# Delta-rule recurrence, soft MoE and FFN in one kernel: keys, queries and values loaded and scattered per step, held by semaphores, instead of per pair of steps

## The chip, the cores and the metric

The kernel runs on one core of a Trainium2 chip. The metric is the device time of one execution in microseconds (us), as the median over runs.

## The reference

Three layers follow each other. The first one is the part that the change touches:

```python
# q, k, v: (4, 8, 768, 48), beta: (4, 8, 768); D = 48, 32 heads in all
k_n = k / (norm(k) + 1e-06)
state = zeros(B, H, D, D)
for t in range(768):
    y[t] = q[t] @ state
    state += beta[t] * outer(k_n[t], v[t] - k_n[t] @ state)
x = y as (3072, 384)
logits = x @ phi                      # 32 slots, 4 for each of 8 experts
d = softmax(logits over the tokens);  slots = d.T @ x
slots[e] = relu(slots[e] @ w1[e]) @ w2[e]
x = softmax(logits over the slots) @ slots
out = max(0.01 * h, h) @ w_out        # with h = x @ w_in
```

## The kernel before

The 768 positions are cut into 24 steps (`NST`) of 32 positions, for all 32 heads at once. Inside a step the recurrence is a triangular system, so that each step is a row of small matrix products with one solve; the solves are made on VectorE (DVE) for four steps at a time (`solve`, six groups), ahead of the steps that use them. The heads are in two halves, A = 0 and A = 1.

**Loads.** The inputs lie in DRAM by pairs of steps. `load_pair(p)` brings keys and queries of two steps, twice: as a block-diagonal operand (`kbd`, in the arena; two scatters of 192 KB, L161) and as a plain one (`kqr`, 768 KB, L162). `gram(s)` multiplies one by the other (L172, 32 small matmuls a step), ScalarE (ACT) copies one half of the product (L178), and DVE masks the other (L183). Grams run eight to ten steps ahead of the step that uses them. `load_kv(p)` brings keys and values of two steps (768 KB, L276). `step_k(p)` scales the keys of both steps on ACT and splits them into two 16-bit parts (L302, L305, L306), and `step_kdma(p)` scatters them into `khb`, the operand of the state's update (four transfers of 96 KB for a pair, L314). `step_dma(s)` scatters the solved matrices into `tmb` (four of 64 KB, L325) and loads `kqb`, keys and queries of one step once more (two of 192 KB, L321).

**One step.** TensorE (PE) forms keys times state (`ks_mm`, L347) into `ksu`, to which the values have been added (L339). ACT and DVE split it (`z_of`, L361 to L363). PE multiplies by the solved matrix (`u_mm`, L369: T z, closed in steps 0 to 16 by a further matmul, L376), ACT reads u (L374, L377), and PE adds keys times u to the state's accumulator in PSUM (`s_mm`, L390: the state's products). ACT reads the new state (L393), which the next step's `ks_mm` needs. The step's output y is queries times state (`qs_mm`, L355) plus L400. This loop from state to state is the chain of a step; grams, the solve of a later group, the outputs' logits and the loads lie beside it.

**What sets the order.** A scheduler orders each engine's instructions ahead of time, by priorities in a table `P`; on the chip each engine runs its list in order and waits on semaphores. All transfers are issued from one queue, SyncE's (SP), in one order; each issue also waits for the transfer eight before it. PE, ACT, DVE, POOL and SP each have a program of their own, and loading of code is done by transfers too (the page calls these queues "instruction").

**Stages.** 0 to 17 us: first loads and a warm-up of PE. 17 to 49 us: grams of steps 0 to 7 and the first solve's start. 49 to 74 us: the first solve on DVE. 78 to 352 us: the 24 steps. 352 to 418 us: the experts' weights arrive. 418 to 647 us: the FFN (L898, L930 to L938), which loads nothing large.

Of the kernel before, what the change touches and what calls it, by code (L numbers as in the profile page):

```python
# [24 lines left out]
ROWS = 3  # L25
GALT = 8
WARM = 28
KB = 2
GR = ((0, 2, 2), (2, 0, 0))
COLS = 2  # L30
NL = 7
# [16 lines left out]
def fused_kernel(ctx: ExitStack, tc: tile.TileContext, kq, kv, bu, phi, w1, w2, wi, wo, out):  # L48
    nc = tc.nc
    ve, sc, gp, pe, sy = nc.vector, nc.scalar, nc.gpsimd, nc.tensor, nc.sync  # L50

    def pool(stack, name, bufs, **kw):
        return stack.enter_context(tc.tile_pool(name=name, bufs=bufs, **kw))
# [7 lines left out]
    p_late = pool(ctx, "late", 2, side="right")  # L61
# [34 lines left out]
    def place(kb, shape, dt):  # L96
# [6 lines left out]
        if len(shape) == 2:  # L103
# [46 lines left out]
    last_dma = [None]  # L150
    kqc, gcs, mms, tcs, nns, kvs, vns = {}, {}, {}, {}, {}, {}, {}

    def load_pair(p):
        n = 4 if p < 4 else 2
        c, kb = kqc[p] = kqr[p % n], kbd[p % n]
        kr = kq[p].rearrange("p k (b x y) -> p k b x y", b=2, x=2)
        cr = c[0:96].rearrange("p k b x i h -> p k (b x i h)")
        for ks in (slice(0, 1), slice(1, 2)) if p == 0 else (slice(0, 2),):
            for sl in range(2):
                q, i = slice(48 * sl, 48 * sl + 48), slice(32 * sl, 32 * sl + 32)  # L160
                last_dma[0] = sy.dma_start(kb[q, ks, :, i].rearrange("p k b i h -> p k b (i h)"), kr[q, ks, :, 0]).ins  # L161
            sy.dma_start(cr[:, ks], kq[p, :, ks])  # L162

    def gram(s):
        k = s % 2
# [104 lines left out]

    solved = {}

    def load_kv(p):
        t = p_late.tile([128, 2, 2, 384], F32, tag=f"kv{p % 2}", name="kv", bufs=1)
        with tc.issue_after(kb_dma[0]) if p < 2 else nullcontext():
            sy.dma_start(t, kv[p])  # L276
        kvs[p] = t

    khs = {}

    def step_m(s):
        g, k = divmod(s, 4)
# [6 lines left out]
    def step_ew(s):  # L289
        g, k = divmod(s, 4)  # L290
        v1 = kvs[s // 2][:, s % 2, 1]
        if s % 2:
            kvs.pop(s // 2)
        vs = p_w.tile([128, 8, 48], F32, tag="vs", name="vs", bufs=3)
        gp.tensor_tensor(vs, v1.rearrange("p (h e) -> p h e", h=8), nns[g][:, k].unsqueeze(2).to_broadcast([128, 8, 48]), MULT)  # L295
        vns[s] = vs

    def step_k(p):
        khc = p_w.tile([128, 2, 2, 384], F16, tag="khc", name="khc", bufs=KB)
        for k in range(1 if p == NST // 2 - 1 else 2):  # L300
            k1 = kvs[p][:, k, 0]
            sc.activation(k1, k1, AF.Copy, scale=64.0)  # L302
            kv1 = k1.rearrange("p (d a h) -> p a d h", a=2, h=4)
            k0, kl = [khc[:, k, l].rearrange("p (a d h) -> p a d h", a=2, h=4) for l in range(2)]
            sc.activation(k0, kv1, AF.Copy)  # L305
            gp.tensor_tensor(kl, kv1, k0, SUB)  # L306
        khs[p] = khc.rearrange("p k l (a x) -> p (k l a) x", a=2)

    def step_kdma(p):
        khc = khs.pop(p)  # L310
        n = 1 if p == NST // 2 - 1 else 2
        for b in range(4):
            q, o = slice(32 * b, 32 * b + 32), 48 * (b % 2)
            last_dma[0] = sy.dma_start(khb[q, 0:n, :, :, b // 2, o:o + 48, :].rearrange("p k l a d h -> p (k l a) (d h)"), khc[q, 0:4 * n]).ins  # L314

    def step_dma(s):
        g, k = divmod(s, 4)
# [11 lines left out]
    sps = [t[:, 0:384].rearrange("p (b h e) -> p b h e", b=2, h=4) for t in spf]  # L329
# [6 lines left out]
    last_u = {}  # L336
# [48 lines left out]
    def s_mm(s, A, u):  # L385
        kb = khb[:, s % 2]
        for hh in range(4):
            for i, (a, b) in enumerate(PASSB):
                for bp in range(2):
                    pe.matmul(sps[A][:, bp, hh, :], kb[:, a, A, bp, :, hh], u[:, b, hh, :],  # L390
                              start=False, stop=(s == NST - 2 and i == 2), skip_group_check=True)
        st = p_s.tile([128, 2, 4, 48], F32, tag=f"s{A}", name="st")
        sc.activation(st.rearrange("p b h e -> p (b h e)"), sps[A].rearrange("p b h e -> p (b h e)"), AF.Copy)  # L393
        S[A] = st
# [170 lines left out]
    wm = ps_m.tile([128, 512], F32, tag="m", name="wm")  # L565
    for i in range(WARM):
        pe.matmul(wm, one16, xg[0][:, 0].rearrange("p a b -> p (a b)")[:, 0:512], start=True, stop=True)
    for p in range(2):
        load_pair(p)
    with tc.issue_after(last_dma[0]):  # L570
        sy.dma_start(beta, bu)
    for s in range(4):
# [1 line left out]
    kb_dma = [last_dma[0]]  # L574
    with tc.issue_after(last_dma[0]):
        load_kv(0)
        phi_sb = p_sm.tile([128, 3, 32], F32, tag="pt", name="phi_sb")
        sy.dma_start(phi_sb, phi)
    sc.activation(phs[:, 0], phi_sb, AF.Copy, scale=64.0)
# [1 line left out]
    late_zero()  # L581
    bs.add(solve(0))
    bs.run(8)
    for p in range(2, 4):
        load_pair(p)
    for p in range(2, 4):
        bs.run(8)
        for t in range(2 * p, 2 * p + 2):
            drain(gram(t))
            bs.run(8)  # L590
    bs.run()
    load_kv(1)
    prep(0)
    step_k(0)
    step_kdma(0)
    step_dma(0)
    prep(1)
    load_pair(4)
    bs.add(solve(1))
    bs.run(DQ[0])  # L600

    for s in range(NST):
        y = ps_y.tile([128, 8, 48], F32, tag="y", name="y")
        z, u = {}, {}
# [49 lines left out]
        if s < NST - 1:  # L654
            with pri("st"):
                s_mm(s, 0, u[0])
# [5 lines left out]
        if s < NST - 1:  # L662
            with pri("st"):
                s_mm(s, 1, u[1])
        if s + 2 < NST:
            if s % 2 and (s + 3) // 2 < NST // 2:
                load_kv((s + 3) // 2)
            with pri("prep"):
                prep(s + 2)
        if s % 2 and s + 1 < NST:  # L670
            with pri("dma"):
                step_kdma((s + 1) // 2)
        if s % 2 == 0 and s + 2 < NST:
            with pri("prep"):
                step_k(s // 2 + 1)
        conv()
        bs.run(dq[6])
        bg.run(GR[s % 2][2])
# [4 lines left out]
        with pri("x"):  # L683
            x = xg[s // 4 % 2][:, s % 4]
# [5 lines left out]
            else:  # L690
                ve.scalar_tensor_tensor(x1, y, 2.0 ** -8, x0, MULT, SUB)
        vns.pop(s)
        if s % 2 == 0 and (s + 10) // 2 < NST // 2:
            with pri("split"):
                load_pair((s + 10) // 2)
        if s % 4 == 2:
            bs.run()
            if s == 14:
# [153 lines left out]
    with tc.high_priority(offset=CHAIN_PRIO):  # L852
# [132 lines left out]
```

## Time and profile before

| | us |
|---|---|
| median of three runs | 650.26 |
| the three runs | 647.53, 650.26, 650.75 |
| the profiled execution's own time | 649.27 |
| its span in the trace | 647.5 |

The page gives the busy time of each engine, the clock that PE was granted, and how the DMA engines were used. The chain of waits follows the last instruction back to what released it; in it "issue" is a stretch in which PE waited for nothing that the trace shows. The timelines show each engine's instructions with the idle time ahead of them and what ended it. The windows give each engine's busy time in a stretch.

### The profile page before, as it was taken

What the parts mean: (1) busy time and instruction counts of PE and PEld (TensorE: products, weight loads), DVE (VectorE), ACT (ScalarE), POOL (GpSimd) and SP (SyncE); (2) the same over time, 40 slices, a digit from 0 to 9 for tenths busy, and PEclk for the clock granted to TensorE, in tenths of its full rate; (3) what the DMA queues carried; (4) which work ended last, traced back from release to release, by engine and by line L of the source; (5) the groups of instructions that cost most, each with busy time, mean ns of one, the idle gap of its engine ahead of it and who ended that gap; (6) DMA issues with size and microseconds to landing.
All of it is one profiled execution on the core that took longest, in us unless ns stands there. A gap on an engine that the chain in (4) does not pass through costs nothing.

```text
span 647.5 us, 21565 instructions
## 1 busy us (share of the span) xinstructions
PE 545.4 (84%) x9171; PEld 388.5 (60%) x9171; DVE 400.0 (62%) x1064; ACT 300.2 (46%) x714; POOL 205.1 (32%) x217
## 2 busy tenths in 40 slices
PE   5651399899999898989777757778999999999996
PEld 2640287778788787878776222345655555555553
DVE  3169988769676797978366895699333333233321
ACT  0322246456456456655343221255565556555652
POOL 9432003023033123131111000054555554555452
PEclk9875599899899899989888687899999999999999
DMA  8972247748475655487969999520010101010101
GB/s 212 256 154 98 35 117 167 169 117 193 101 157 125 148 119 133 84 222 157 258 167 364 416 412 416 204 97 1 1 51 0 50 1 50 0 51 1 50 1 49
DMA packets 67184, 87.46 MB, mean 135 GB/s; under 512 B 41520, under 2 KB 58160, under 8 KB 66032
## 3 DMA queue, kind: packets, MB, share of 16 engines
q1 hardware_dynamic: 67088, 86.09, 48.0%
q8 instruction: 72, 1.18, 0.8%
q14 instruction: 24, 0.20, 0.1%
HBM read 70.53 MB, written 4.72 MB: 116 GB/s over the span
## 4 chain that ended last, share of the span: by engine, by line
PE 65%; DMA 12%; DVE 12%; issue 6%; ACT 2%; SPq 1%; POOL 0%; DVEq 0%; ACTq 0%
PE ops L898 27%; PE gm L172 7%; PE sps L390 5%; PE y L355 4%; PE ksu L347 4%; PE hps L930 3%; PE ksu L369 3%; PE y L400 3%; DMA we<-in_w_dram 2%; PE ksu L339 2%; DMA arena<-in_w_dram 2%; DMA arena<-in_kq_dram 2%; DMA khb<-khc 2%; DVE arena L256 2%; DVE arena L242 2%
## 5 line engine op out<-in xcount | busy, mean ns | idle before, releaser
L938 POOL TENSOR_TENSOR gl<-gf,gh 128x512 f16<-128x512 f32 x96 | 114.0, 1204 | 171.2 <-ACT gh L937 100.8
L898 PE MATMUL ops<-late,gh 128*128 128x384 f16 x768 | 143.6, 326 | 0.3 <-ACT gh L937 0.3
L936 DVE SCALAR_TENSOR_TENSOR gf<-hps,hs 128x512 f32<-128x512 f32 x96 | 62.2, 686 | 112.6 <-ACT hs L935 107.5
L898 PEld LDWEIGHTS <-gh 128*128 128x128 f16 x768 | 74.9, 98 | 56.6 <-ACT gh L937 3.0
L898 PE MATMUL ops<-late,gl 128*128 128x384 f16 x384 | 81.2, 326 | 1.6 <-POOL gl L938 1.5
L172 PE MATMUL gm<-kqr,arena 128*32 128x64 f32 x1280 | 56.0, 309 | 29.4 <-DVE er L213 24.6
L935 ACT ACTIVATE hs<-hps 128x512 f32<-128x512 f32 x96 | 52.4, 594 | 51.9 <-PE hps L930 51.9
L937 ACT ACTIVATE gh<-gf 128x512 f16<-128x512 f32 x96 | 60.3, 630 | 32.5 <-DVE gf L936 27.3
L295 POOL TENSOR_TENSOR vs<-kv,nn 128x384 f32<-128x384 f32 x24 | 21.8, 913 | 145.1 <-PE ksu L339 117.2
L172 PEld LDWEIGHTS gm<-kqr,arena 128*32 128x32 f32 x1280 | 43.3, 150 | 35.3 <-DVE er L213 25.1
L390 PE MATMUL sps<-u,khb 128*128 128x48 f16 x1104 | 52.7, 195 | 5.5 <-issue 2.1
L256 DVE TENSOR_TENSOR arena<-arena 128x81 f32<-128x81 f32 (+12 forms) x150 | 55.7, 371 | 0.2
L390 PEld LDWEIGHTS <-khb 128*128 128x128 f16 x1104 | 46.6, 118 | 11.8 <-issue 10.2
L898 PEld LDWEIGHTS <-gl 128*128 128x128 f16 x384 | 37.4, 98 | 26.8 <-POOL gl L938 2.4
L260 DVE TENSOR_TENSOR arena<-arena 128x81 f32<-128x81 f32 (+12 forms) x150 | 49.7, 331 | 0.0
L242 DVE SCALAR_TENSOR_TENSOR arena<-arena 128x28 f32<-128x28 f32 (+27 forms) x186 | 49.2, 275 | 0.4
L355 PE MATMUL y<-st,kqb 128*32 128x48 f32 x1472 | 39.7, 233 | 1.0 <-issue 1.0
L347 PE MATMUL ksu<-st,kqb 128*32 128x48 f32 x1472 | 37.3, 233 | 3.3 <-issue 2.4
L347 PEld LDWEIGHTS ksu<-st,kqb 128*32 128x32 f32 x1472 | 30.8, 158 | 9.8 <-issue 6.1
L393 ACT ACTIVATE st<-sps 128x384 f32<-128x384 f32 x46 | 22.4, 490 | 29.8 <-PE sps L390 29.7
L369 PE MATMUL ksu<-z,tmb 128*128 128x48 f16 x576 | 28.7, 193 | 8.7 <-issue 7.8
L306 POOL TENSOR_TENSOR khc<-kv,khc 128x384 f16<-128x384 f32 x23 | 21.4, 952 | 45.9 <-ACT khc L305 45.9
(171 smaller groups left out, 891.6 us busy)
## 6 DMA issues: line engine op xcount, KB each, us to landing
we<-in_w_dram SPq DMA_DIRECT2D x22, 768.0 KB, 13.5
kqb<-in_kq_dram SPq DMA_DIRECT2D x50, 192.0 KB, 5.4
kv<-in_kv_dram SPq DMA_DIRECT2D x12, 768.0 KB, 7.2
arena<-in_w_dram SPq DMA_DIRECT2D x10, 768.0 KB, 11.9
kqr<-in_kq_dram SPq DMA_DIRECT2D x9, 768.0 KB, 7.8
tmb<-tc SPq DMA_DIRECT2D x96, 64.0 KB, 3.3
arena<-in_wi_dram SPq DMA_DIRECT2D x8, 768.0 KB, 7.6
raw<-in_wo_dram SPq DMA_DIRECT2D x8, 768.0 KB, 9.2
```

What stands on the lines that cost most here:

```text
L172: pe.matmul(gm[32 * b:32 * b + 32, h, :], kb[:, k, bp, r, h], c[:, k, bp, :, :, h], start=(h == 0), stop=True, skip_group_check=True)
L242: ve.scalar_tensor_tensor(R[:, i, 0:j], R[:, j, 0:j], gu[:, i, j:j + 1], R[:, i, 0:j], MULT, ADD)
L256: ve.tensor_tensor(tv, gu[:, j + 2:, j:j + 1].to_broadcast([128, n, w]), R[:, j:j + 1, 0:w].to_broadcast([128, n, w]), MULT)
L260: ve.tensor_tensor(R[:, j + 2:, 0:w], R[:, j + 2:, 0:w], tv, ADD)
L347: pe.matmul(ksu[A][32 * b:32 * b + 32, 48 * hh:48 * hh + 48], kb[:, bp, 0, r, 4 * A + hh], st[:, bp, hh, :], start=False, stop=True, skip_ ...
L355: pe.matmul(y[32 * b:32 * b + 32, 4 * A + hh, :], kb[:, bp, 1, r, 4 * A + hh], st[:, bp, hh, :], start=(A == 0 and hh == 0), stop=False, s ...
L390: pe.matmul(sps[A][:, bp, hh, :], kb[:, a, A, bp, :, hh], u[:, b, hh, :], start=False, stop=(s == NST - 2 and i == 2), skip_group_check=True)
L898: pe.matmul(ops[t], g[:, 128 * t:128 * t + 128], w, start=(ft == 0 and i == 0), stop=(ft == 15 and i == 2))
L935: sc.activation(hs, hps, AF.Copy, scale=2.0 ** -12)
L936: ve.scalar_tensor_tensor(gf, hps, 0.01 * 2.0 ** -12, hs, MULT, MAX)
L937: sc.activation(gh, gf, AF.Copy)
L938: gp.tensor_tensor(gl, gf, gh, SUB)
```

## The change

Everything that was loaded for a pair of steps is loaded for one step, with half the size and the same sum of bytes: `load_pair` becomes `load_kq` (two scatters of 96 KB and one load of 384 KB for a step), `load_kv` takes one step (384 KB), and `step_k` and `step_kdma` treat one step (four scatters of 48 KB). In the loop the scatters for step s+10 wait for the last product of the state in step s (`s_mm`, half 1), and the values of step s+3 wait for the last matmul of T z in step s (`u_mm`, half 0). `khc` gets a third buffer, each half as large. Before the loop, the second `step_k` is made ahead of the first step. Matmuls, ACT and DVE instructions are the same in number; SP issues 88 transfers more.

```diff
-KB = 2
+KB = 3
...
-    def load_pair(p):
+    def hold(dma, ins):
+        tc.add_manual_dep(dma.ins, ins.name, mybir.DependencyInfo(mybir.DependencyClass.Sync, mybir.DependencyReason.DATA), reason="hold")
+
+    def load_kq(s, ins=None):
+        p, k = divmod(s, 2)
         n = 4 if p < 4 else 2
-        c, kb = kqc[p] = kqr[p % n], kbd[p % n]
...
+        for sl in range(2):
+            q, i = slice(48 * sl, 48 * sl + 48), slice(32 * sl, 32 * sl + 32)
+            d = sy.dma_start(kb[q, k, :, i].rearrange("p b i h -> p b (i h)"),
+                             kq[p, q, k].rearrange("p (b x y) -> p b x y", b=2, x=2)[:, :, 0])
+            if ins is not None:
+                hold(d, ins)
+            last_dma[0] = d.ins
+        sy.dma_start(c[0:96, k].rearrange("p b x i h -> p (b x i h)"), kq[p, :, k])
...
-    def load_kv(p):
-        t = p_late.tile([128, 2, 2, 384], F32, tag=f"kv{p % 2}", name="kv", bufs=1)
-        with tc.issue_after(kb_dma[0]) if p < 2 else nullcontext():
-            sy.dma_start(t, kv[p])
-        kvs[p] = t
+    def load_kv(s, ins=None):
+        p, k = divmod(s, 2)
+        if k == 0:
+            kvs[p] = p_late.tile([128, 2, 2, 384], F32, tag=f"kv{p % 2}", name="kv", bufs=1)
+        d = sy.dma_start(kvs[p][:, k], kv[p, :, k])
+        if ins is not None:
+            hold(d, ins)
...
-    for p in range(2, 4):
-        load_pair(p)
+    for t in range(4, 8):
+        load_kq(t)
...
-    load_kv(1)
+    load_kv(2)
     prep(0)
     step_k(0)
     step_kdma(0)
     step_dma(0)
     prep(1)
-    load_pair(4)
+    step_k(1)
+    load_kq(8)
+    load_kq(9)
...
+        if s + 3 < NST:
+            load_kv(s + 3, last_u[0].ins)
         if s + 2 < NST:
-            if s % 2 and (s + 3) // 2 < NST // 2:
-                load_kv((s + 3) // 2)
             with pri("prep"):
                 prep(s + 2)
-        if s % 2 and s + 1 < NST:
+        if s + 1 < NST - 1:
             with pri("dma"):
-                step_kdma((s + 1) // 2)
-        if s % 2 == 0 and s + 2 < NST:
+                step_kdma(s + 1)
+        if s + 2 < NST - 1:
             with pri("prep"):
-                step_k(s // 2 + 1)
+                step_k(s + 2)
+        if s + 10 < NST:
+            load_kq(s + 10, last_s[0])
...
-        if s % 2 == 0 and (s + 10) // 2 < NST // 2:
-            with pri("split"):
-                load_pair((s + 10) // 2)
```

The change moves instructions at three places. In the rows below the lines of the changed kernel are higher: L185 was L178 (copy of a gram), L190 was L183 (mask of a gram), L216 was L209, L220 to L223 were L213 to L216, L230 was L223 (rows of the solve), L308 and L311 were L302 and L305 (keys), L366 and L367 were L361 and L362 (z), L379 and L382 were L374 and L377 (u), L398 was L393 (state), L319 was L314, L326 was L321, L330 was L325, L164 was L161 and L284 was L276 (transfers).

DVE, start of the first solve, before (`mm` is a masked gram, `er`, `br` and `arena` belong to the solve):

```order
L202 STREAM_TRANSPOSE arena<-arena 128x1024
L209 TENSOR_SCALAR t_367<-arena 128x32
L183 TENSOR_TENSOR mm<-gm,causal 128x2x4x32 x2
L213 TENSOR_SCALAR er<-nu 128x32
L233 RECIPROCAL ru<-nu 128x32
L214 TENSOR_TENSOR er<-er,arena 128x32
L215 RECIPROCAL er<-er 128x32
L183 TENSOR_TENSOR mm<-gm,causal 128x2x4x32
L216 SCALAR_TENSOR_TENSOR br<-er,beta 128x32
L217 TENSOR_SCALAR arena<-br 128x32
L223 TENSOR_TENSOR arena<-arena,br 128x16x16
```

and in the change:

```order
L209 STREAM_TRANSPOSE arena<-arena 128x1024
L216 TENSOR_SCALAR t_371<-arena 128x32
L190 TENSOR_TENSOR mm<-gm,causal 128x2x4x32
L220 TENSOR_SCALAR er<-nu 128x32
L240 RECIPROCAL ru<-nu 128x32
L221 TENSOR_TENSOR er<-er,arena 128x32
L190 TENSOR_TENSOR mm<-gm,causal 128x2x4x32
L222 RECIPROCAL er<-er 128x32
L223 SCALAR_TENSOR_TENSOR br<-er,beta 128x32
L224 TENSOR_SCALAR arena<-br 128x32
L230 TENSOR_TENSOR arena<-arena,br 128x16x16
```

Ahead of `br` there stand two masks where there were three: the third, of gram 6, now comes after four rows L230.

SP in two steady steps, before (a step of a pair with the values' load, then one with the keys' scatter):

```order
L325 DMA tmb_73<-tc 32x8x128 x4
L321 DMA kqb_72<-in_kq_dram 48x4x256 x2
L314 DMA khb<-khc 32x8x192 x4
L325 DMA tmb_74<-tc 32x8x128 x4
L276 DMA kv<-in_kv_dram 128x1536
```

and in the change, one step:

```order
L319 DMA khb<-khc 32x4x192
L164 DMA arena<-in_kq_dram 48x2x256 x2
L330 DMA tmb_74<-tc 32x8x128 x4
L284 DMA kv<-in_kv_dram 128x768
L319 DMA khb<-khc 32x4x192 x3
L326 DMA kqb_71<-in_kq_dram 48x4x256 x2
```

The scatters into the arena now stand directly behind the first of the four `khb` transfers and ahead of the matrices and the values of the same step.

ACT at one step's end, before (`sps_153` and `sps_154` are the accumulators of the state's two halves):

```order
L393 ACTIVATE st<-sps_153 128x384
L211 ACTIVATE nu<-nu 128x32
L393 ACTIVATE st<-sps_154 128x384
L686 ACTIVATE xg_128<-y 128x384
L302 ACTIVATE kv<-kv 128x384 x2
L361 ACTIVATE z<-ksu_157 128x192
```

and in the change:

```order
L398 ACTIVATE st<-sps_153 128x384
L382 ACTIVATE u<-ksu_158 128x192
L308 ACTIVATE kv<-kv 128x384
L311 ACTIVATE khc<-kv 128x384
L366 ACTIVATE z<-ksu_157 128x192
L367 ACTIVATE z<-ksu_157 128x192
L398 ACTIVATE st<-sps_154 128x384
```

The scaling of the keys, one instruction in each step instead of two in every second one, has moved ahead of the second half's state.

## Rows read from the trace of the kernel before

**Rows 1.** Page, part 1: busy time of each engine.

```profile
PE 545.4 (84%) x9171; PEld 388.5 (60%) x9171; DVE 400.0 (62%) x1064; ACT 300.2 (46%) x714; POOL 205.1 (32%) x217
```

**Rows 2.** Windows: stretch, length, busy time (count) of PE, PEld, DVE, ACT, POOL; clock; DMA share, GB/s.

```profile
17.00:49.00 32.00, 19.32 (x576) 18.21 (x576) 12.89 (x34) 10.59 (x31) 12.52 (x17) 0.84 0.92 202
107.30:121.20 13.90, 11.14 (x317) 9.38 (x315) 10.08 (x28) 7.62 (x23) 1.40 (x2) 0.88 0.80 184
146.30:158.70 12.40, 12.40 (x374) 11.28 (x372) 11.60 (x35) 8.39 (x26) 5.47 (x7) 1.00 0.76 167
158.70:172.90 14.20, 11.76 (x305) 9.76 (x305) 9.16 (x40) 6.56 (x20) 0.90 (x2) 0.88 0.45 116
209.10:223.00 13.90, 11.81 (x315) 10.21 (x313) 9.29 (x44) 6.17 (x17) 1.33 (x2) 0.88 0.72 172
233.90:247.20 13.30, 12.67 (x314) 10.64 (x312) 9.52 (x41) 6.81 (x22) 3.02 (x6) 1.00 0.41 83
```

**Rows 3.** Chain of waits: start us, length us, what.

```profile
23.52 2.48 issue
30.24 4.83 issue
39.30 2.92 issue
114.92 1.81 issue
117.24 1.66 PE gm L172 x46
160.86 2.44 issue
163.30 0.84 PE ksu L347 x35
215.64 2.09 issue
```

**Rows 4.** DMA view, 112 to 115 us: queues with packets, MB, share.

```profile
q1 hardware_dynamic: 710, 0.79, 100.1%
q8 instruction: 1, 0.02, 2.2%
```

**Rows 5.** Timeline of ACT: start, length, work, count [idle before <-releaser].

```profile
117.06 0.95 ACT L302 ACTIVATE kv<-kv 128x384 f32<-128x384 f32 x2 [2.94 <-DMA kv<-in_kv_dram]
121.19 0.49 ACT L393 ACTIVATE st<-sps 128x384 f32<-128x384 f32 x1 [0.34 <-PE sps L390]
218.02 0.94 ACT L302 ACTIVATE kv<-kv 128x384 f32<-128x384 f32 x2 [4.30 <-DMA kv<-in_kv_dram]
```

**Rows 6.** Timelines of DVE (first row) and PE (the others).

```profile
43.10 0.69 DVE L183 TENSOR_TENSOR mm<-gm,causal 128x256 f32<-128x256 f32 x1 [3.37 <-ACT arena L178]
119.25 0.49 PE L376 MATMUL ksu<-u,n 128*128 128x192 f16 x2
130.30 0.19 PE L390 MATMUL sps<-u,khb 128*128 128x48 f16 x1 [0.63 <-DMA khb<-khc]
```

**Rows 7.** Timeline of SP: DMA issues, start and length of issuing.

```profile
105.45 0.58 SPq L162 DMA_DIRECT2D kqr<-in_kq_dram  x1
106.13 0.37 SPq L276 DMA_DIRECT2D kv<-in_kv_dram  x1
145.50 1.28 SPq L161 DMA_DIRECT2D arena<-in_kq_dram  x2
248.17 1.93 SPq L314 DMA_DIRECT2D khb<-khc  x3
```

**Rows 8.** DMA views of several stretches: count, KB each, median us to landing.

```profile
kv<-in_kv_dram SPq DMA_DIRECT2D x1, 768.0 KB, 6.5
kqr<-in_kq_dram SPq DMA_DIRECT2D x2, 384.0 KB, 4.0
khb<-khc SPq DMA_DIRECT2D x4, 96.0 KB, 2.3
```

More of the change, by code (lines that the diff above doesn't have):

```diff
@@ L151, in fused_kernel @@
     kqc, gcs, mms, tcs, nns, kvs, vns = {}, {}, {}, {}, {}, {}, {}
-    def load_pair(p):
+    def hold(dma, ins):
+        tc.add_manual_dep(dma.ins, ins.name, mybir.DependencyInfo(mybir.DependencyClass.Sync, mybir.DependencyReason.DATA), reason="hold")
+    def load_kq(s, ins=None):
+        p, k = divmod(s, 2)
         n = 4 if p < 4 else 2
-        c, kb = kqc[p] = kqr[p % n], kbd[p % n]
[L156 to L162, printed above, removed]
+        if k == 0:
+            kqc[p] = kqr[p % n], kbd[p % n]
+        c, kb = kqc[p]
+        for sl in range(2):
[6 more added lines that the diff above has]
+        sy.dma_start(c[0:96, k].rearrange("p b x i h -> p (b x i h)"), kq[p, :, k])
     def gram(s):
@@ L271, in fused_kernel @@
     solved = {}
-    def load_kv(p):
-        t = p_late.tile([128, 2, 2, 384], F32, tag=f"kv{p % 2}", name="kv", bufs=1)
-        with tc.issue_after(kb_dma[0]) if p < 2 else nullcontext():
-            sy.dma_start(t, kv[p])
-        kvs[p] = t
-    khs = {}
+    def load_kv(s, ins=None):
+        p, k = divmod(s, 2)
+        if k == 0:
+            kvs[p] = p_late.tile([128, 2, 2, 384], F32, tag=f"kv{p % 2}", name="kv", bufs=1)
+        d = sy.dma_start(kvs[p][:, k], kv[p, :, k])
+        if ins is not None:
+            hold(d, ins)
+    khs, last_s = {}, [None]
     def step_m(s):
@@ L291, in step_ew @@
         v1 = kvs[s // 2][:, s % 2, 1]
-        if s % 2:
-            kvs.pop(s // 2)
         vs = p_w.tile([128, 8, 48], F32, tag="vs", name="vs", bufs=3)
@@ L296, in step_ew, with step_k, step_kdma @@
         vns[s] = vs
[L298 to L311, printed above, removed]
+    def step_k(s):
+        khc = p_w.tile([128, 2, 384], F16, tag="khc", name="khc", bufs=KB)
+        k1 = kvs[s // 2][:, s % 2, 0]
+        sc.activation(k1, k1, AF.Copy, scale=64.0)
+        kv1 = k1.rearrange("p (d a h) -> p a d h", a=2, h=4)
+        k0, kl = [khc[:, l].rearrange("p (a d h) -> p a d h", a=2, h=4) for l in range(2)]
+        sc.activation(k0, kv1, AF.Copy)
+        gp.tensor_tensor(kl, kv1, k0, SUB)
+        khs[s] = khc.rearrange("p l (a x) -> p (l a) x", a=2)
+    def step_kdma(s):
+        khc = khs.pop(s)
         for b in range(4):
             q, o = slice(32 * b, 32 * b + 32), 48 * (b % 2)
-            last_dma[0] = sy.dma_start(khb[q, 0:n, :, :, b // 2, o:o + 48, :].rearrange("p k l a d h -> p (k l a) (d h)"), khc[q, 0:4 * n]).ins
+            last_dma[0] = sy.dma_start(khb[q, s % 2, :, :, b // 2, o:o + 48, :].rearrange("p l a d h -> p (l a) (d h)"), khc[q]).ins
     def step_dma(s):
@@ L389, in s_mm @@
                 for bp in range(2):
-                    pe.matmul(sps[A][:, bp, hh, :], kb[:, a, A, bp, :, hh], u[:, b, hh, :],
-                              start=False, stop=(s == NST - 2 and i == 2), skip_group_check=True)
+                    last_s[0] = pe.matmul(sps[A][:, bp, hh, :], kb[:, a, A, bp, :, hh], u[:, b, hh, :],
+                              start=False, stop=(s == NST - 2 and i == 2), skip_group_check=True).ins
         st = p_s.tile([128, 2, 4, 48], F32, tag=f"s{A}", name="st")
@@ L567, in fused_kernel @@
         pe.matmul(wm, one16, xg[0][:, 0].rearrange("p a b -> p (a b)")[:, 0:512], start=True, stop=True)
-    for p in range(2):
-        load_pair(p)
+    for t in range(4):
+        load_kq(t)
     with tc.issue_after(last_dma[0]):
@@ L576, in fused_kernel @@
         load_kv(0)
+        load_kv(1)
         phi_sb = p_sm.tile([128, 3, 32], F32, tag="pt", name="phi_sb")
@@ L583, in fused_kernel @@
     bs.run(8)
-    for p in range(2, 4):
-        load_pair(p)
+    for t in range(4, 8):
+        load_kq(t)
     for p in range(2, 4):
```

## The prediction

> **What bounds the kernel now.** I read the page's busy times first: PE is busy for 545.4 us, 84% of the span [rows 1]. So the time is PE's work plus its holes, and the change leaves PE's work as it is. What counts is which holes it closes or opens. The windows show where they are [rows 2]: in the first grams (17 to 49 us) PE is busy for 19.3 of 32.0 us with the DMA engines at 0.92. A step in the loop that runs clean takes 12.4 us with PE busy all of it (146.30 to 158.70). Three steps take 13.9, 14.2 and 13.9 us, with 2.1 to 2.8 us of holes and the clock at 0.88, and one takes 13.3 us.
>
> The chain of waits names the holes. At 23.52, 30.24 and 39.30 us it shows "issue" of 2.48, 4.83 and 2.92 us, and in the three long steps 1.81, 2.44 and 2.09 us [rows 3]: PE waited there for no data. The DMA view around the first of the three steps shows the usual queue filling the engines to 100.1% and one packet on the instruction queue [rows 4]. The other two have such a packet too, and PE goes on soon after it. I read the holes as PE's code coming late, behind bulk data. The timeline of SP shows which bulk: 768 KB for kqr at 105.45 us and 768 KB for kv at 106.13 us, back to back [rows 7]; two such bursts more go ahead of the other two steps. ACT's timeline shows the same bursts from another side: the keys' scaling (L302) waits for its values for 2.94 and 4.30 us in two of those steps [rows 5], and smaller waits of the kind lie between.
>
> **The change part by part.**
>
> *The start.* The bytes are the same, but the first scatter has five loads of 384 KB ahead of it (1.9 MB) where it had two of 384 and three of 768 KB (3.1 MB), ACT treats one step of values ahead of grams 2 and 3 instead of two, and the mask of gram 6, which kept DVE waiting for 3.37 us ahead of the solve's `br` [rows 6], comes after it. If the code comes as late as now, what is left is one L302 with its copy L305 (0.95 us for two such, [rows 5]) and one mask of 0.69 us that no longer stands ahead of `br`: -1.6. Without the wait ahead of that mask it is 3.37 more: -5.0. If the hole at 23.52 us, which delays the grams of this solve itself, goes as well, 2.48 more [rows 3]: -7.4. I take -5.0, because the wait belongs to an instruction that has moved away, while the first hole only shrinks: the eight transfers that SP may have under way are of at most 384 KB each where they were of up to 768. The solve that follows ends the stage, so a gain here shifts all that comes after it.
>
> *The holes in the loop.* With 384 KB loads held until a point of the step, the two bursts of one moment no longer meet. By the holes the three steps give 1.81 + 2.44 + 2.09 = 6.3; the step of 233.90 us gives 13.3 - 12.4 = 0.9 [rows 2], and the wait for `khb` 0.63 [rows 6]: 7.9. By step lengths against 12.4 us it is 1.5 + 1.8 + 1.5 + 0.9 + 0.6 = 6.3. I take -7.0.
>
> *New: the held scatter.* The gram of step s+10 follows the last product of step s in PE's order, and its first matmul waits for the scatter. In eight of the fourteen held grams (10, 12, 13, 15, 16, 20, 21 and 23) only 2.1 to 3.6 us of matmuls stand between, summed at the dense rates 1.66 us for 46 and 0.84 us for 35 [rows 3]; in the other six 6.1 us or more. Behind the hold SP issues one `khb` transfer (1.93 / 3 = 0.64 us) and the first scatter (1.28 / 2 = 0.64) [rows 7], and 96 KB land in 2.3 us [rows 8]: 3.6 us. So each of the eight waits about 0.05 to 1.5 us, 5.4 in all. At least 2 (gram work moves into later gaps), at most 12.6, if each scatter waits behind half of a 384 KB load. I take +4.5.
>
> *New: the held values.* ACT now scales the keys of step s+3 right after the first half's state and ahead of the second half's. Their load is held on the last T z matmul of half 0, at t0. In the first of the long steps t0 is at the row at 119.25 us, and the first state is ready at 121.19 + 0.49 = 121.7, so ACT comes to L302 at t0 + 2.4 [rows 5, 6]. The load needs 0.37 us of issue [rows 7] and about 4.0 us for 384 KB; 768 KB took 6.5 [rows 8]: it lands at t0 + 4.1 to 4.4. ACT thus stands for some 2 us with the second state behind it. The second state's first reader is half 1 of the next `ks_mm`; ahead of that PE has half 0, the values' product and part of a gram. Laid against each other in six steps this covers a landing at up to t0 + 4.5 and costs 0 to 0.5 us a step before that; below, nothing, at the top 16. I take +3.0.
>
> *The rest.* The 88 further issues cost SP 0.4 to 0.64 us each; SP's program has room for them (see the rivals). Scaling and splitting keys per step is the same ACT work. From 285 us on the stream of weights sets the holes; there the half loads swap places with weights, which I put at 0, within 3 either way. The FFN is unchanged and only shifts.
>
> *The sum:* -5.0 - 7.0 + 4.5 + 3.0 = -4.5 on the profiled execution's own 649.27 us: 644.8. The median is 1.0 above that execution (650.26 against 649.27), so I predict 645.8.
>
> One rule speaks of the holes. The Trainium skill (Runtime: NRT & Kernel Launch, Instruction fetch mechanics) has code come in by a DMA queue of its own, with the refill mostly hidden behind what is executed. Here it is not hidden: by that rule the holes would have another cause, which smaller loads need not touch; what that makes of the sum stands with the second rival.
>
> **The rivals.** A measurement of this kernel tells about 0.5% from no change: faster is below 647.0, slower above 653.5.
>
> *All waits go.* If half-size loads let the code through everywhere, and scatters hide: -7.4 - 7.9 + 2 + 0 = -13.3, so 637.0. For it: the holes do coincide with the bursts. Against it: eight grams are very near to their scatters. Chance 0.13.
>
> *What is gained is given back.* The start stays as it is for code (-1.6), the loop's three holes halve with the loads (6.3 / 2 = 3.2) and the 0.9 goes, scatters cost 4.5 and values 3: +1.8, so 652.1. For it: at the start the sum of bytes is the same and the engines are full (0.92 [rows 2]), so less ahead of the code need not mean that it comes sooner. Chance 0.20. Within it, with 0.04, the holes have another cause than the loads and stay whole: -1.6 - 0.9 - 0.6 + 4.5 + 3 = +4.4, so 654.7. That is where the Trainium skill's rule on instruction fetch (above) would lead.
>
> *Slower: the held values come late.* If a 384 KB load lands at t0 + 5.25 instead of 4.4, each of some 20 steps pays 0.75 more, since ACT keeps the second state behind L302: -4.5 + 15 = +10.5, so 660.8. It decides from t0 + 4.5 on; at t0 + 4.75 the whole gain is gone. For it: the load now starts together with three `khb` transfers and two of `kqb` right behind it on SP, and the wait stands on the chain's own engine. Against it: 384 KB landed in 4.0 us even as two at once [rows 8]. Chance 0.14.
>
> *Slower: issuing on SP.* A step now issues 14 transfers: two scatters, one load of keys, one of values, four `khb`, four `tmb`, two `kqb`, about 14 x 0.6 = 8.4 us of 12.4. In the last steps, which have no gram and are shorter, that leaves little, and with in-order holds a `kqb` or `tmb` comes late: by an estimate of two issues (2 x 0.6) in each of eight steps, 9.6 in all: -4.5 + 9.6 = +5.1, so 655.4. Chance 0.05. The Trainium skill (DMA: Bandwidth & Descriptors, Measured) asks for batches of 1 MiB or more, against many small ones, and so speaks against the whole change. The rows agree that halving does not halve the landing (6.5 us for 768 KB, 4.0 for 384 KB [rows 8]), but it is the large loads here that keep PE waiting.
>
> **How the numbers follow.** The forecast has 0.48, with a range of its own of 641 to 649 (each term's ends, not all at once); of it 0.42 lies below 647.0 and 0.06 above. Faster: 0.42 + 0.13 = 0.55. Same: 0.06 + 0.16 of the second rival = 0.22. Slower: 0.04 + 0.14 + 0.05 = 0.23. The range runs from 637, the first rival's own time (half of its chance, 0.07, lies below), to 657, below most of the late values' rival (0.10 of its 0.14 lies above): 0.17 is left out.
>
> **What the changed profile would show.** The "issue" pieces at the start get shorter and the first transpose of the solve (now L209) comes earlier; no 2 us "issue" in steps 3, 7 and 11; L308 on ACT waits 1.5 to 2 us in nearly every step for its values, with the second state (L398) right behind it; the first gram matmul (L179) in eight steps waits about 1 us for DMA; step lengths near 12.4 us throughout. I am wrong if the holes stay with smaller loads (then code is late for another reason), if L308 ends later than PE needs the second state in most steps (time above 653), or if `tmb` or `kqb` appears as what ends PE's waits (SP's order is the bound).

## The result: 0.3 to 1.1% faster

The changed kernel took 650.11 us as a median of 12 runs, against 652.59 us of the kernel before, also 12. The ratio is 0.989, with a 95% interval of 0.9845 to 0.9936. Single executions of one kernel lie up to 2.4% apart (640.39 to 655.85 us for the changed one, 647.53 to 655.81 for the one before), and the ratio leaves out those over 1.5% above their kernel's fastest, which are six of the changed kernel's and none of the other's, so that it leans towards a gain. The plain medians give 0.996. A second comparison of the same two kernels, 12 runs against 23, gave 0.9967 (0.9932 to 1.0002), and 0.996 by plain medians. So the gain is 2 to 7 us, and the second comparison does not exclude that there is none. The forecast of 4.5 us (0.993) lies within this. The median itself, 650.11 us, is 4.3 above the 645.8 forecast, in part because the kernel before took 652.59 us here, not 650.26. By the prediction's own bounds of 0.5% the first ratio is "faster" (chance 0.55), the second and both plain medians are "same" (0.22).

The terms of the forecast did much worse than its sum. The changed kernel's profiled execution took 649.97 us, 0.7 more than that of the kernel before, and this is how it is made up, from the first and last rows of the state's copies (L393 before, L398 after) in ACT's timeline (the first row of each kernel stands above the table):

```profile
82.60 0.49 ACT L393 ACTIVATE st<-sps 128x384 f32<-128x384 f32 x1 [0.80 <-PE sps L390]
```

```profile
72.19 0.49 ACT L398 ACTIVATE st<-sps 128x384 f32<-128x384 f32 x1 [0.64 <-PE sps L395]
```

| stretch, us | before | changed | changed, 2nd profile |
|---|---|---|---|
| start to the first state | 82.6 | 72.2 | 71.1 |
| from there to the first state of step 15 | 185.6 | 193.3 | 194.9 |
| from there to the last state | 76.3 | 79.9 | 79.5 |
| the rest to the end of the span | 303.1 | 302.9 | 306.3 |
| span | 647.5 | 648.2 | 651.8 |

The start gained 10.4 us and the loop gave back 11.3. PE's busy time stayed: 546.3 us on the page's first part, against 545.4 [rows 1].

```profile
PE 546.3 (84%) x9171; PEld 389.9 (60%) x9171; DVE 392.7 (61%) x1064; ACT 301.6 (47%) x714; POOL 203.4 (31%) x217
...
q8 instruction: 72, 1.18, 0.9%
```

The windows of the changed kernel (columns as in [rows 2]): the first grams, then three steps between first states.

```profile
17.00:49.00 32.00, 18.73 (x512) 16.92 (x504) 19.77 (x60) 10.90 (x33) 13.37 (x17) 0.83 0.85 184
98.30:112.70 14.40, 11.15 (x299) 9.51 (x297) 10.61 (x36) 7.25 (x20) 2.34 (x3) 0.88 0.67 147
125.80:139.10 13.30, 12.82 (x344) 11.40 (x342) 9.71 (x34) 7.70 (x22) 4.08 (x5) 1.00 0.56 120
152.80:164.10 11.30, 10.24 (x293) 8.90 (x290) 7.15 (x26) 6.97 (x20) 3.99 (x6) 1.00 0.58 135
```

In the start PE does no more than before, but DVE is busy for 19.8 us where it was for 12.9. In the loop a step of 14.4 us has 3.3 us of holes and the clock at 0.88, like the long steps before. What stands in the holes has changed. The chain of waits of the changed kernel, between 75 and 317 us:

```profile
99.65 5.83 DMA arena<-in_kq_dram
...
116.31 3.66 DMA arena<-in_kq_dram
...
142.95 4.57 DMA arena<-in_kq_dram
...
193.22 6.28 DMA arena<-in_kq_dram
...
316.24 1.21 issue
```

The "issue" pieces of [rows 3] are gone up to 316 us, but for one of 0.46 us at 304.88, and the held scatters stand in their place: those shown took 3.7 to 6.3 us from issue to landing. The waits of PE from 72 to 333 us say the same in sums (total, times, longest); the first fence is the changed kernel, the second the kernel before:

```profile
PE gm L179 <- DMA arena<-in_kq_dram: 8.9, 5, 3.3
PE xp L413 <- ACT xg L699: 4.0, 2, 3.1
PE y L698 <- ACT xg L696: 2.9, 1, 2.9
PE ksu L374 <- DVE z L368: 2.5, 3, 1.6
```

```profile
PE ksu L369 <- issue: 5.6, 3, 2.1
...
PE xp L408 <- ACT xg L689: 0.9, 1, 0.9
...
PE ksu L369 <- DVE z L363: 0.3, 1, 0.3
PE y L688 <- ACT xg L686: 0.2, 1, 0.2
```

The last three rows of the first fence are the held values. ACT's timeline of the changed kernel shows why: the copy of the output (`xg`) and the next z stand behind the scaling of the keys (L308), which waits for its load.

```profile
77.16 0.52 ACT L308 ACTIVATE kv<-kv 128x384 f32<-128x384 f32 x1 [3.54 <-DMA kv<-in_kv_dram]
77.59 0.47 ACT L696 ACTIVATE xg<-y 128x384 f16<-128x384 f32 x1
...
280.87 0.52 ACT L308 ACTIVATE kv<-kv 128x384 f32<-128x384 f32 x1 [3.65 <-DMA kv<-in_kv_dram]
281.43 0.52 ACT L311 ACTIVATE khc<-kv 128x384 f16<-128x384 f32 x1
281.86 0.31 ACT L366 ACTIVATE z<-ksu 128x192 f16<-128x192 f32 x1
282.07 0.32 ACT L367 ACTIVATE z<-ksu 128x192 f16<-128x192 f32 x1
282.28 0.49 ACT L699 ACTIVATE xg<-y 128x384 f16<-128x384 f32 x1
```

PE waits until 78.11 us for the first `xg` and until 282.83 us for the last.

### The profile page after: what moved, and what is told of

Same layout as the page of the kernel before. It is cut to its first block, busy times and chain, and to the rows that moved or that the text cites. A ratio compares the mean times of both kernels' runs of the same rounds, so it can differ in the third digit from the quotient of the medians.

```text
span 648.2 us, 21698 instructions
## 1 busy us (share of the span) xinstructions
PE 546.3 (84%) x9171; PEld 389.9 (60%) x9171; DVE 392.7 (61%) x1064; ACT 301.6 (47%) x714; POOL 203.4 (31%) x217
## 4 chain that ended last, share of the span: by engine, by line
PE 63%; DMA 16%; DVE 15%; issue 3%; ACT 2%; SPq 1%; POOL 0%; DVEq 0%; ACTq 0%; POOLq 0%
PE ops L905 26%; PE gm L179 6%; PE sps L395 5%; DMA arena<-in_kq_dram 5%; PE y L360 5%; DMA kv<-in_kv_dram 3%; PE hps L937 3%; PE ksu L374 3%; PE ksu L352 3%; PE y L405 3%; PE ksu L344 2%; DMA arena<-in_w_dram 2%; PE son L824 1%; PE xp L413 1%; DVE arena L263 1%
## 5 line engine op out<-in xcount | busy, mean ns | idle before, releaser
L945 POOL TENSOR_TENSOR gl<-gf,gh 128x512 f16<-128x512 f32 x96 | 112.6, 1190 | 161.0 <-ACT gh L944 88.7
L179 PE MATMUL gm<-kqr,arena 128*32 128x64 f32 x1280 | 57.3, 308 | 36.4 <-DVE er L220 23.0
L302 POOL TENSOR_TENSOR vs<-kv,nn 128x384 f32<-128x384 f32 x24 | 19.9, 834 | 149.4 <-DMA kv<-in_kv_dram 59.7
L395 PE MATMUL sps<-u,khb 128*128 128x48 f16 x1104 | 50.6, 196 | 1.4 <-ACT u L382 1.2
L395 PEld LDWEIGHTS <-khb 128*128 128x128 f16 x1104 | 45.1, 118 | 5.8 <-issue 4.2
L249 DVE SCALAR_TENSOR_TENSOR arena<-arena 128x28 f32<-128x28 f32 (+27 forms) x186 | 44.8, 250 | 0.4
L352 PE MATMUL ksu<-st,kqb 128*32 128x48 f32 x1472 | 39.6, 231 | 0.9 <-issue 0.8
L352 PEld LDWEIGHTS ksu<-st,kqb 128*32 128x32 f32 x1472 | 33.9, 156 | 10.2 <-issue 8.0
L398 ACT ACTIVATE st<-sps 128x384 f32<-128x384 f32 x46 | 22.5, 490 | 28.7 <-PE sps L395 28.3
L360 PEld LDWEIGHTS y<-st,kqb 128*32 128x32 f32 x1472 | 32.2, 159 | 5.3 <-issue 1.5
L190 DVE TENSOR_TENSOR mm<-gm,causal 128x256 f32<-128x256 f32 x24 | 15.6, 657 | 31.1 <-ACT arena L185 30.8
```

The source lines that it names most:

```text
L179: pe.matmul(gm[32 * b:32 * b + 32, h, :], kb[:, k, bp, r, h], c[:, k, bp, :, :, h], start=(h == 0), stop=True, skip_group_check=True)
L249: ve.scalar_tensor_tensor(R[:, i, 0:j], R[:, j, 0:j], gu[:, i, j:j + 1], R[:, i, 0:j], MULT, ADD)
L352: pe.matmul(ksu[A][32 * b:32 * b + 32, 48 * hh:48 * hh + 48], kb[:, bp, 0, r, 4 * A + hh], st[:, bp, hh, :], start=False, stop=True, skip_ ...
L360: pe.matmul(y[32 * b:32 * b + 32, 4 * A + hh, :], kb[:, bp, 1, r, 4 * A + hh], st[:, bp, hh, :], start=(A == 0 and hh == 0), stop=False, s ...
L395: last_s[0] = pe.matmul(sps[A][:, bp, hh, :], kb[:, a, A, bp, :, hh], u[:, b, hh, :], start=False, stop=(s == NST - 2 and i == 2), skip_gr ...
L945: gp.tensor_tensor(gl, gf, gh, SUB)
```

## The experiments

Each edit also lets the scheduler make another order, so that kernels differ by more than the edit. The experiments ran on three chips, and each kernel has one profile (the changed one two), which need not be a typical run of it. A few us in one stretch are therefore no proof; I rely on stretches and on waits that appear or vanish in several kernels. All ratios are against the kernel before, run on the same chip. The stretches of all of them stand in one table behind the last one.

**The changed kernel again** (no edit).

> The changed kernel once more, unedited, for a second profile of it. Theory A (the gain comes from the first loads: the first profile has the first state 10.4 us earlier, at 72.2 instead of 82.6 us; the loop's closed holes are given back in waits of the grams for the held scatters, 8.9 us, and of ACT for the held values): the first state again at 71 to 74 us, no issue of 2 us in the loop before 300 us, gram waits of 6 to 11 us. Theory B (the early start is an accident of that execution and the gain lies in the loop): first state at 77 to 83 us and the loop from first state to step 22 at most 250 us. Time against before: 0.985 to 0.997.

Measured: 0.9967, first state at 71.1 us, 8.4 us of gram waits for scatters. Two "issue" pieces are there in the loop (1.32 us at 99.84, 2.47 at 195.70), so the holes are fewer, not excluded. The stretches fit theory A in that the start is the gain and the loop the loss.

**The first loads of keys and queries per step, alone**, in the kernel before:

```diff
-    for p in range(2):
-        load_pair(p)
+    for t in range(4):
+        load_kq(t)
...
-    for p in range(2, 4):
-        load_pair(p)
+    for t in range(4, 8):
+        load_kq(t)
```

> The kernel before with only the eight steps ahead of the loop loading keys and queries per step; the loop loads pairs as before. Theory A: most of the early start shows (first state at 72 to 77 us) and the time falls by 4 to 9 us against before (0.986 to 0.994), with the loop's three issue holes still there. Theory B: first state within 2 us of 82.6, time the same as before within 0.4%.

Measured: 0.9867 (0.9813 to 0.992), first state at 75.7 us, the loop with its issue holes (1.89 us at 107.78, 2.59 at 154.47) at 186.5 us. This half of the start gives 6.9 us by itself.

**The changed kernel with the old first loads**: the same lines the other way round, and the first pair of values in one transfer.

> The changed kernel with the old first loads: keys and queries of steps 0 to 7 by pairs, and the first pair of values in one transfer; the loop as changed. Theory A: first state at 80 to 84 us again, the loop without issue holes but with gram waits of 6 to 11 us, time against before 0.998 to 1.008. Theory B: time against before 0.985 to 0.995 all the same.

Measured: 0.9986 (0.9946 to 1.0026), but the first state at 72.1 us. The ratio is just inside theory A's range, but its interval holds the changed kernel's 0.9967 too, and the plain medians on this chip are the same (647.82 and 647.65 us). The place went against theory A: the start kept its gain with the old loads of 768 KB, in the changed kernel's order of work. So the size of the first loads is not needed for it.

**The changed kernel without both holds**:

```diff
-            load_kv(s + 3, last_u[0].ins)
+            load_kv(s + 3)
...
-            load_kq(s + 10, last_s[0])
+            load_kq(s + 10)
```

> The changed kernel without both holds in the loop; loads per step go as soon as their buffers are free and the scheduler puts them in the queue. Theory A: the gram waits fall from 8.9 us to under 3 and ACT's waits for values from 19 us to under 8, and the loop gets 4 to 9 us shorter unless the loads then meet PE's code again: time against before 0.975 to 0.990. Rival (the holds are what keeps the code's transfers clear): issue holes of 2 us come back in the loop, two or more of them, and the time is 0.990 to 1.003 of before.

Measured: 0.9756 (0.9701 to 0.9811), a median of 635.46 us. No gram waits for a scatter, one issue piece (0.83 us at 141.51) stands in the chain between 75 and 297 us (one of 2.2 us is among PE's waits, off the chain), and the two stretches of the loop take 180.4 and 74.2 us. The rival fell: it is not the holds that keep the holes away. Splitting (of the loads in the start and in the loop) is the gain, holding is the loss. One part of the expectation missed: ACT's waits for values fell to 13.6 us, not under 8.

**Each hold alone taken away** (one of the two lines above).

> The changed kernel without the hold on the scatters (keys and queries); the values stay held. The two profiles of the changed kernel show 8.9 and 8.4 us of gram matmuls waiting for scatters and 19.3 and 11.8 us of ACT waiting for values. Theory A1 (the scatters' hold is the main loss): gram waits under 2 us and 0.974 to 0.986 of before. Theory A2 (the values' hold is the main loss, since ACT has the second state behind it): 0.986 to 0.996.

> The changed kernel without the hold on the values; the scatters stay held. A1: gram waits of 6 to 11 us stay and the time is 0.986 to 0.996 of before. A2: 0.974 to 0.986. If neither hold alone explains the 0.9756 of the kernel without both, both this and the other kernel lie near 0.985.

Measured: without the scatters' hold 0.9893 (0.9853 to 0.9933), without the values' hold 0.9928 (0.9896 to 0.9961). Neither theory holds alone; it is the last sentence of the second expectation that comes near. The stretches separate them: without the scatters' hold the steps up to 15 take 176.5 us instead of 193.3, but the late ones 82.9; without the values' hold the early steps stay at 191.6 and the late ones take 76.2. The values' hold has a second place, in step 0. ACT's timeline of the kernel that holds the values only:

```profile
76.79 0.52 ACT L308 ACTIVATE kv<-kv 128x384 f32<-128x384 f32 x1 [3.66 <-DMA kv<-in_kv_dram]
77.22 0.47 ACT L398 ACTIVATE st<-sps 128x384 f32<-128x384 f32 x1
...
78.00 0.48 ACT L398 ACTIVATE st<-sps 128x384 f32<-128x384 f32 x1
```

Here both halves of the first state stand behind the wait, which is why its first state comes at 77.2 us.

**How near the scatter's hold lies to its gram.** The hold for step s+10 on the last product of step s-1 (first), and on the last T z matmul of half 1 of step s (second):

```diff
-            load_kq(s + 10, last_s[0])
+            load_kq(s + 10, prev_s)
```

```diff
-            load_kq(s + 10, last_s[0])
+            load_kq(s + 10, last_u[1].ins)
```

> The changed kernel with the scatters for step s+10 held on the last product of the state of step s-1 instead of step s; values held as changed. Measured so far, from the first state to the first state of step 15: 193.3 and 194.9 us with both holds, 176.5 with only the values held, 185.6 in the kernel before. Theory L (the hold costs because the scatter starts too near to its gram; a hold with a step of lead costs little): gram waits for scatters under 2 us in all, this stretch 176 to 184 us. Rival (holds cost because SP stands at them and all that is queued behind comes late, wherever they are): stretch 188 us or more.

> The changed kernel with the scatters for step s+10 held on the last T z matmul of half 1 of step s, some 2 us ahead of the last product of the state. Theory L: between both: gram waits of 1 to 5 us instead of 8.9 and 8.4, and 180 to 190 us from the first state to that of step 15. Rival as for the hold a step earlier: 190 us or more.

Measured: a step earlier 0.9894 (0.9835 to 0.9953), some 2 us earlier 0.9869 (0.9828 to 0.991). The waits of PE from 72 to 333 us, first with the hold at the T z matmul, then a step earlier:

```profile
PE gm L179 <- DMA arena<-in_kq_dram: 1.7, 2, 1.3
```

```profile
PE gm L179 <- DMA arena<-in_kq_dram: 0.4, 1, 0.4
```

Waits of 8.9, 1.7, 0.4 and none go with early stretches of 193.3, 185.4, 182.1 and 176.5 us, and the kernels with waits of 4.7 and 6.8 us in the table below (191.6 and 190.8) fit between. So the traces bear out theory L: it is the lead that counts, and a hold costs little where its transfer has a step in hand. The runs do not tell the three longer leads apart: 0.9869, 0.9894 and, without this hold, 0.9893.

**The values held in steps 0 to 13 only**, the scatters not at all:

```diff
-            load_kv(s + 3, last_u[0].ins)
+            load_kv(s + 3, last_u[0].ins if s < 14 else None)
```

> The changed kernel without the hold on scatters, and with the hold on values only in steps 0 to 13. From step 15's first state to the last state it measured 79.9, 79.5 and 82.9 us with values held (both holds twice, values only), 74.2 and 76.2 without. Theory K (the values' hold costs in the late steps, which have no gram and are short, not in the early ones): this stretch 73 to 77 us, the stretch before it 175 to 181 us, and 0.972 to 0.982 of before. Rival (the values' hold costs nothing of its own, the late stretch differs by the weights' loads): 79 us or more.

Measured: 0.981 (0.9766 to 0.9855), late stretch 74.0 us, early 180.2, as theory K says; how far the late stretch scatters without any hold stands below the table. The first state came at 80.4 us, behind a wait of 4.10 us for values as shown above.

**Keys and queries by pairs in the loop, no hold**: the pair's load stands at its old place, values and `khb` per step.

```diff
-        if s + 10 < NST:
-            load_kq(s + 10, last_s[0])
...
+        if s % 2 == 0 and (s + 10) // 2 < NST // 2:
+            with pri("split"):
+                load_pair((s + 10) // 2)
```

> The changed kernel without holds and with keys and queries loaded by pairs in the loop, as before; values, and the keys' operand of the state, per step. Theory S (the loop's issue holes go with the smaller loads, without any hold): one or two issue holes over 1 us between 100 and 290 us, where the kernel before has four and the kernel without holds none, and 181 to 188 us from the first state to that of step 15, against 180.4 without holds. Rival (the holes went with the loads of values alone): no such hole, 177 to 182 us.

Measured: 0.9883 (0.9833 to 0.9934). Theory S fell: with loads of 768 KB for keys and queries there is no issue piece of 0.7 us or more in the chain from 75 to 290 us. The rival is right about the holes and wrong about the time: the early stretch is 185.7 us, no shorter than before. In place of the holes, PE waits between 72 and 333 us for z (2.4 us), for the state (2.1) and for the copies of the output (3.8).

**The scaling of the first keys behind the grams' copies on ACT**, in the kernel before (first), and in the one without holds, together with the scaling of phi (second); `g7` is the copy of gram 7:

```diff
-    step_k(0)
+    with tc.issue_after(g7):
+        step_k(0)
```

> The kernel before, all loads by pairs, with one edit: the scaling of the first keys on ACT is put behind the copy of gram 7, so that the grams' copies do not stand behind a wait for values. Theory C (the start's gain is ACT's order, not the sizes of the loads: kernels with either half of the new start had the first state at 72 to 76 us): the second transpose of the solve moves from 71.5 to 63 to 67 us, the loop keeps its issue holes, time 0.984 to 0.993 of before. Rival (code late behind bulk loads sets the start): no more than 2 us earlier, 0.996 to 1.002.

> The changed kernel without both holds, and with the scaling of the first keys behind the copy of gram 7 and the scaling of phi behind that of gram 3, on ACT and DVE. Theory C: the gram copies no longer wait for values (6 us of waiting at 28 us goes), the first state falls from 75 to 66 to 70 us and the time to 0.962 to 0.970 of before. Rival: first state within 2 us of 75, time 0.973 to 0.978.

Measured: 0.9998 (0.996 to 1.0036) and 0.9783 (0.9736 to 0.9831). Theory C fell in both. In the kernel before, the first transpose of the solve came 3.9 us earlier and its end 0.3 us earlier. Its chain, DVE's timeline and POOL's (last row) show what took the place of the wait:

```profile
29.96 5.12 issue
```

```profile
28.99 2.01 DVE L202 STREAM_TRANSPOSE arena<-arena 128x1024 f32<-128x1024 f32 x1
...
35.91 0.68 DVE L183 TENSOR_TENSOR mm<-gm,causal 128x256 f32<-128x256 f32 x1 [4.70 <-ACT arena L178]
...
46.48 0.78 DVE L256 TENSOR_TENSOR arena<-arena 128x81 f32<-128x81 f32 x1
47.19 0.86 DVE L242 SCALAR_TENSOR_TENSOR arena<-arena 128x3 f32<-128x3 f32 x1
...
70.07 1.25 DVE L263 STREAM_TRANSPOSE arena<-arena 128x1024 f32<-128x1024 f32 x1
```

```profile
47.12 0.91 POOL L306 TENSOR_TENSOR khc<-kv,khc 128x384 f16<-128x384 f32 x1
```

PE's hole without data to wait for is there as before, of 5.12 us instead of 4.83 [rows 3], and the solve, started sooner, stood at the next mask. That took 0.5 us of the 3.9: the solve's first row L256 still came 3.4 us earlier (46.48 instead of 49.88). The other 3.1 us went between this row and the solve's end, a stretch of 23.6 us instead of 20.5 with 0.1 us of idle time on DVE. The rows of L256 and L242 in it took 20.8 us instead of 17.7: the splitting of the keys on POOL (L306) had moved beside them, and the last section shows what that does. The second kernel has the same: against the kernel without holds the first row came 3.1 us earlier, the end 0.3 us.

The stretches of all kernels (us; columns as in the first table), and the gram waits for scatters:

| kernel | first state | to step 15 | to the last | gram waits |
|---|---|---|---|---|
| before | 82.6 | 185.6 | 76.3 | none |
| changed | 72.2 | 193.3 | 79.9 | 8.9 |
| changed again | 71.1 | 194.9 | 79.5 | 8.4 |
| first loads per step, alone | 75.7 | 186.5 | 79.9 | none |
| changed, old first loads | 72.1 | 190.8 | 79.1 | 6.8 |
| no holds | 75.1 | 180.4 | 74.2 | none |
| values held only | 77.2 | 176.5 | 82.9 | none |
| scatters held only | 74.6 | 191.6 | 76.2 | 4.7 |
| scatters held a step earlier | 72.7 | 182.1 | 77.9 | 0.4 |
| scatters held at T z | 70.7 | 185.4 | 81.7 | 1.7 |
| values held to step 13 | 80.4 | 180.2 | 74.0 | none |
| pairs of keys, no holds | 75.2 | 185.7 | 73.9 | none |
| before, keys' scaling late | 82.3 | 189.2 | 73.5 | none |
| no holds, scaling late | 74.8 | 177.1 | 73.3 | none |

The late stretch scatters too: the kernel before's own loop, which holds nothing, gave 76.3, 79.9 and 73.5 us. The six profiles of changed kernels that hold the values there have 77.9 to 82.9, the five that don't 73.3 to 76.2.

The best version measured is the changed kernel without holds: 2.4% faster than the kernel before, and faster than the changed kernel by intervals that do not meet. The versions with the late scaling and with the values held to step 13 are the same within their intervals.

## Why the sum held and its terms did not

The sum was -4.5; the runs gave -2 to -7, so sign, size and range came out. That terms as wrong as these add up to it is luck. By the profiled executions its terms were -5.0 (measured -10.4), then -7.0 + 4.5 + 3.0 = +0.5 for the loop (measured +7.7 and +3.6), and 0 for the rest (measured -0.2). Two errors of about 5 and 11 us stood against each other. These two executions lie 0.7 us apart, the medians 2.5.

**The start, -5.0: right sign, half the size.** From the first transpose of the solve to its last one it took 37.5 us before and 30.0 after (the changed kernel first):

```profile
31.77 2.31 DVE L209 STREAM_TRANSPOSE arena<-arena 128x1024 f32<-128x1024 f32 x1
...
61.82 1.25 DVE L270 STREAM_TRANSPOSE arena<-arena 128x1024 f32<-128x1024 f32 x1
```

```profile
32.91 1.92 DVE L202 STREAM_TRANSPOSE arena<-arena 128x1024 f32<-128x1024 f32 x1
...
70.36 1.25 DVE L263 STREAM_TRANSPOSE arena<-arena 128x1024 f32<-128x1024 f32 x1
```

That is 7.4; the first transpose came 1.1 us earlier, and from the second row to the first state it took 1.9 less: 10.4. Of the 7.4, 5.2 are waits of DVE for grams. My term had one of them, the 3.37 us of [rows 6]; two more of 1.33 and 0.79 us stood ahead of the masks of grams 5 and 4, and of all three 0.29 us is left. Another 1.6 us are rows of the solve that got shorter (last section). The reason that I gave, less data ahead of PE's code, is not shown. PE's "issue" idle time from 17 to 45 us did fall, from 10.3 us to 1.3 (2.7 in the second profile). But with the old loads it is 3.2 us and the gain stays (72.1), and with the first loads per step alone it is 9.8 us (3.3 of them behind these grams) and most of the gain is there (75.7); in that kernel the first gram starts at 13.8 us instead of 17.0. Nor is it the order of the masks: that last kernel has three of them ahead of `br`, as before, with 1.30 us of waiting for the last. Freeing ACT alone gives no gain (82.3). What the changed kernel, the two just named and the one without holds share is that ACT's copy of gram 6, which that mask waits for, starts at 35.3 to 37.1 us, not at 42.7 (40.8 with ACT freed alone). Either half of the edit does that alone; how is not settled.

**The holes, -7.0: gone, but not worth that.** Between 80 and 290 us PE's "issue" idle time fell from 7.8 us to 0.4 (2.7 in the second profile). The holes went, though not because of the size of the keys' loads: with pairs of 768 KB and values per step they go as well (1.0 us). That fits my reason, the meeting of two large loads. But a meeting alone makes no hole. The prediction counts three in the kernel before, and SP's timeline has a fourth:

```profile
180.31 0.60 SPq L162 DMA_DIRECT2D kqr<-in_kq_dram  x1
182.01 0.43 SPq L276 DMA_DIRECT2D kv<-in_kv_dram  x1
```

Two packets of the instruction queue fall between 184 and 190 us, with the usual queue at 102.1%, and from 178 to 196 us PE is busy for all 18.00 us. The page still has 72 packets on the instruction queue, as before. The step that failed is the price: a hole that goes leaves PE at the next wait. In the kernel with pairs and no holes the stretch is as long as before (185.7 and 185.6 us); 3 to 9 us came only where the loads were per step and the scatters free or held a step ahead (182.1, 180.4, 180.2, 177.1 and 176.5). That code arrives late behind bulk data stays a reading of the rows, in which the holes went when loads moved; it was not tried by itself.

**The scatters, +4.5: half the size, from the wrong row.** I let the 96 KB land in 2.3 us, as `khb` did [rows 8], which is a copy of 96 KB from one place on the chip to another. The scatter reads DRAM, and `khb` and `tmb` follow it at once on SP. The row was also the best case: `khb` in the kernel before took 2.3 to 7.3 us from 72 to 300 us, half of them more than 2.8. The 28 scatters took 2.1 to 6.3 us, half of them more than 3.2, and the slow ones made the price: in five steps, not eight, the gram waited 3.25, 2.29, 2.06, 0.84 and 0.45 us, where I had at most 1.5. The 8.9 us lie within the bounds I gave (2 to 12.6). Without this hold the early stretch falls by 16.8 us (193.3 to 176.5); what beside the 8.9 makes that up, waits further on and the other order, was not taken apart.

**The values, +3.0: right sign, other place.** I expected a wait of some 2 us on ACT in nearly every step, with the second state behind it. There were 12 waits, 19.3 us in all, up to 4.0 us, most with time to spare; behind the dear ones stood the output's copy, z, and in step 0 of two kernels both states. Their price is best seen in the steps from 15 on, which form no grams: not holding the values there took the stretch from 79.9 to 76.2 us with the scatters held, and from 82.9 to 74.0 without. As one and the same loop took 73.5 to 79.9 us there, this price of some 4 to 9 us is no more than an order of size.

**The rivals.** SP's order did not become the bound (no wait of PE from 72 to 333 us ends with `tmb` or `kqb`; the second profile has 1.5 us for `kqb`), and of the late values' rival there is a trace in three waits of over 3.5 us, not in some 20 steps. The profiled execution looks like the second rival (gained, then given back), with other terms: the start did gain, and the scatters took it.

## What to carry to other kernels

A transfer that is held to a point of the program should be held a whole step ahead of its reader, not a few us: here 0.4 us of waits against 8.9, though 2 us more lead already brought it to 1.7 and measured no slower. Splitting a burst and holding its parts are two edits; measured apart, splitting alone gave 2.4% and the holds took more than half of it back. When a hole closes, look for the next wait of that engine before you book the whole hole as a gain, and take a landing time from transfers with the same source and the same neighbours in the queue, with the slowest and not only the median.

## What was not expected of the hardware

DVE's instructions got longer beside POOL's. The same instruction of the solve (209 columns) in the kernel before and in the changed one, from DVE's timelines, with the POOL row that stood beside the first:

```profile
56.27 1.08 DVE L256 TENSOR_TENSOR arena<-arena 128x209 f32<-128x209 f32 x1
```

```profile
56.15 1.96 POOL L306 TENSOR_TENSOR khc<-kv,khc 128x384 f16<-128x384 f32 x2 [4.49 <-ACT khc L305]
```

```profile
49.08 0.37 DVE L263 TENSOR_TENSOR arena<-arena 128x209 f32<-128x209 f32 x1
```

With two POOL instructions on the same stretch it took 1.08 us instead of 0.37, and the next one on DVE 0.87 instead of 0.22. The 25 rows of this line took 10.1 us before, 8.8 in the changed kernel, whose POOL had split the keys earlier, 10.4 in the kernel without holds and with late scaling, whose POOL did five of these splits during the solve, and 11.3 in the kernel before with late scaling. The Trainium skill (SBUF — State Buffer, SBUF: two separate sides) says that a DVE instruction with two inputs from SBUF and a GpSimd instruction that reads SBUF lock each other out for a whole instruction, whichever starts first. These rows agree: in the kernel before, the three L256 rows that began while POOL was at work took 0.79, 0.92 and 1.08 us, where rows of the same size take 0.23, 0.25 and 0.36 later in that solve, and a row that had begun before POOL's kept its length (0.35 us at 55.99). So moving work of ACT and POOL out of the way ahead of the solve, and into it, gave nothing: the two lines L256 and L242 alone took 3.2 us more in the kernel before with late scaling than without, and the same two lines 3.0 us more in the kernel without holds.
